# Attention per head over all 768 queries of a batch, ahead of the experts' first lot

## The chip, the cores and the metric

The kernel runs on one core of one Trainium2 chip. The metric is the device time of one execution in microseconds; the times below are medians of several executions, and one more execution was taken by the hardware profiler, from which all rows come.

## What is computed

Clustered attention feeds two expert networks, one behind the other, all in float32:

```python
# q, k, v: (2 batches, 8 heads, 768, 64); centroids: (8, 16, 64)
q_assign = argmax(q_n @ c_n)              # the cluster of each query, k_assign alike
mask = q_assign[:, :, :, None] == k_assign[:, :, None, :]
scores = where(mask, scale * q @ k.T, -1e9)
attn = softmax(scores);  out = attn @ v
x = out.transpose(0, 2, 1, 3).reshape(1536, 512)
h = x @ w_in                              # 512 -> 2048
g = (a0 + a1*h + a2*h2 + a3*h3) / (1 + |b0|*|h| + |b1|*h2 + 1e-6)
x = g @ w_out                             # 2048 -> 512
h = (x @ w1) * (x @ w2) @ w3              # 512 -> 1024, 1024 -> 1024
return h @ w_out2                         # 1024 -> 512
```

## The kernel before

The 1536 tokens go through in four **lots** of 384 (`c` = 0 to 3; lots 0 and 1 are the two halves of batch 0). The work of a lot is:

- **Masks** (`masks`, one call for a batch): for the keys and then for the queries, squares, norms, products with the centroids and the choice of the cluster, 32x32 transposes on DVE, and a write of the mask rows to DRAM (`msk_d`). Each half of it has six DVE instructions over 128x768.
- **Attention** (`Attn`): `prep` loads a head's q and k (tile `kqr`) and splits them into two float32r parts, tiles `A` and `B`; 16 rows of `B` are mask rows from `msk_d`. `unit` takes 128 queries against all 768 keys: four score matmuls (L802), the negated maximum on DVE (L814), the exponential on ACT (L815), six transposes on PE in two lots of three (L842), each copied out by ACT (L845). A lot has 8 heads times 3 units, so the program has 96 units. `av` (L876) multiplies by v for a pair of heads, two heads side by side in the 128 columns, and divides by the sums; the result goes to `x_d` in DRAM.
- **p1** (L623 to 669): x from `x_d`, times a block of w_in, then the rational function, ten to twelve ACT and DVE instructions of 128x768 (L654 to 668) on a tile `T` of the class `et`. **p2**: w_out. **p3**: w1 and w2 and their product, into tiles of the class `ab`. **p4**: the product w3·w_out2, which the kernel computes itself at its start (**W**: `FirstW` and four `w_block`, L590 and L606, kept in DRAM as `whd`, `wld`).

Every block of weights is used once a lot. In lot 0, p1 and p2 multiply in plain float32 (kind "D", L545), and the weights, which arrive as 64-bit words, are decoded by one ACT and three DVE instructions a half block (L466 to 470) and written back as float32. In the other lots a block is loaded from there into the class `raw` (3 slots), split into two float32r parts (L501 on ACT, L502 on DVE), and each product is three float32r matmuls (L547 to 549).

Lots 0 and 2 load q and k, split k, and write k's two parts to DRAM (`k_d`, L787, L788); lots 1 and 3 read them from there (L780, L781) and load only their own q. v is loaded again for each lot. For lots 1 to 3 `av` splits x into two parts before it writes them to `x_d` (L894, L895), and p1 loads both.

All of it is planned when the program is built: `Plan` places tasks by costs and priorities and gives each buffer a slot of its class (`SLOTS`), so the order on each engine is fixed in advance, and all DMAs stand in one queue, SP's, where an entry waits for its semaphores before the next is issued. Priorities come from `windows`: in before, the planner wants 36 units along with the first W blocks, lot 0's p1 from there on, and each later lot's attention spread under the blocks of the lot ahead of it. Lot 0's p1 needs only lot 0's 24 units.

Of the kernel before, what the change touches and what calls it, by code (L numbers as in the profile page):

```python
# [13 lines left out]
ALU = mybir.AluOpType  # L14
# [7 lines left out]
    F0=('in', 'out'),  # L22
    KEEP=(),
    NORM=(4, 4, 4, 4),
    NW=(1, 4),
    AT=(1.5, 2.2083, 2.5833, 4.0, 4.0, 4.0, 4.0, 4.0, 4.0),
    M1=1,
    LEAD=(5.9, 35.7, 45.3),
    ALEAD=(23.9, 20.0),
    MLEAD=252.0,  # L30
    AOFF=3.7,
    SLOTS={'w': 6, 'raw': 3, 'y': 3, 'x': 2, 'ab': 4, 'x2': 2, 'g': 16, 'et': 3, 'E': 4, 'kqr': 1, 'A': 2, 'B': 2, 'v': 1, 'sm': 6, 'nn': 3, 's': 2, 't': 2, 'm': 2, 'sums': 2, 'rb': 1},
    WO2=-768.4,
    OFF=(-119.7, -2.0, -111.7, -148.2, -107.1, 30.6, -19.2),
    T0=-75.0,
    M0=-37.2,
# [1040 lines left out]
```

## Time and profile before

| | |
|---|---|
| median of 3 runs | 808.32 us (805.76, 808.32, 809.25) |
| the profiled execution | 805.77 us, span 804.0 us |
| PE busy | 775.6 us |
| DVE busy | 614.1 us |
| ACT busy | 555.8 us |
| DMA moved | 172.08 MB, mean 214 GB/s |

Busy time is the union of an engine's instructions. Matmuls overlap their successors, so a PE that is busy all the time is not for that reason at its highest rate; the start-to-start time of equal matmuls tells the rate. Idle time of an engine counts only where the last finisher waits for it.

### The profile page before, as it was taken

Reading aid. Unit: us, or ns where it says so; the run is one execution under the profiler, and the core shown is the slowest. Engines: PE = TensorE matmul, PEld = TensorE weight load, DVE = VectorE, ACT = ScalarE, POOL = GpSimd, SP = SyncE. Lnnn points to the kernel's source line nnn. Section 1 sums busy time; section 2 is a strip of 40 time slices with the busy share of each in tenths; the row PEclk is TensorE's granted clock in tenths of the full one; section 3 lists DMA queues with packets and bytes.
Section 4 is the critical chain, followed back from the end, with each engine's and each line's share of the span. In section 5 each row is a group of like instructions: output and inputs, shape, how many; then the busy total and the mean of one; then the engine's idle time right before and its main releaser. Section 6 shows DMA issues by size and latency. Waiting matters only on the chain.

```text
span 804.0 us, 11696 instructions
## 1 busy us (share of the span) xinstructions
PE 775.6 (96%) x4225; PEld 636.7 (79%) x4225; DVE 614.1 (76%) x842; ACT 555.8 (69%) x959; POOL 0.7 (0%) x6
## 2 busy tenths in 40 slices
PE   3998999998999999999999999999999999999998
PEld 1346655565665768888889889899999999999998
DVE  6988887659999987989999663299994399983440
ACT  4887877778797867899898755378763388663331
POOL 0000000000000000000000000000000000000000
PEclk9999999999999999999999999999999999999999
DMA  8998899998768499666777842243557343653324
GB/s 322 367 304 265 272 293 262 294 284 269 233 174 295 135 368 315 206 207 216 224 234 234 286 161 97 87 132 105 206 199 229 105 134 130 228 178 132 132 103 146
DMA packets 67641, 172.08 MB, mean 214 GB/s; under 512 B 7680, under 2 KB 29952, under 8 KB 67584
## 3 DMA queue, kind: packets, MB, share of 16 engines
q1 hardware_dynamic: 67584, 171.34, 65.2%
q8 instruction: 33, 0.54, 0.3%
q14 instruction: 24, 0.20, 0.1%
HBM read 134.88 MB, written 33.29 MB: 209 GB/s over the span
## 4 chain that ended last, share of the span: by engine, by line
PE 81%; DMA 10%; ACT 4%; DVE 3%; issue 1%; SPq 1%; ACTq 0%; DVEq 0%
PE m L547 12%; PE m L548 12%; PE m L549 12%; PE s L802 6%; PE t L842 6%; PE t L876 6%; PE m L545 5%; DMA raw<-in_w_in_dram 4%; PE s L547 4%; PE s L545 4%; PE s L549 4%; PE s L548 4%; PE m L606 2%; PE t L590 1%; DMA raw<-fin 1%
## 5 line engine op out<-in xcount | busy, mean ns | idle before, releaser
L502 DVE TENSOR_TENSOR w<-raw,w 128x1024 fp32r<-128x1024 f32 x72 | 87.9, 1222 | 60.8 <-ACT w L501 55.2
L501 ACT CAST w<-raw 128x1024 fp32r<-128x1024 f32 x72 | 75.8, 1053 | 82.0 <-PE m L548 59.7
L814 DVE TENSOR_REDUCE sm<-s 128x1 f32<-128x768 f32 x96 | 90.7, 951 | 16.9 <-PE s L802 15.9
L845 ACT COPY et<-t 128x384 f32<-128x384 f32 x192 | 87.8, 494 | 21.6 <-PE t L842 19.5
L815 ACT ACTIVATE E<-s,sm 128x768 f32<-128x768 f32 x96 | 88.2, 920 | 12.5 <-DVE sm L814 10.7
L842 PEld LDWEIGHTS t<-ident,E 128*128 128x128 f32 x576 | 68.8, 140 | 34.1 <-issue 12.1
L842 PE MATMUL t<-ident,E 128*128 128x128 f32 x576 | 86.6, 276 | 7.7 <-ACT et L845 4.4
L547 PE MATMUL m<-x,w 128*128 128x384 f32 x256 | 87.4, 341 | 0.0
L548 PE MATMUL m<-x,w 128*128 128x384 f32 x256 | 86.2, 337 | 0.0
L549 PE MATMUL m<-x,w 128*128 128x384 f32 x256 | 86.1, 336 | 0.0
L876 PE MATMUL t<-et,v 128*64 128x384 f32 x384 | 69.0, 494 | 0.0
L547 PE MATMUL s<-x,w 128*128 128x384 f32 x192 | 66.1, 345 | 0.0
L547 PE MATMUL m<-g,w 128*128 128x384 f32 x192 | 64.9, 338 | 0.0
L549 PE MATMUL s<-x,w 128*128 128x384 f32 x192 | 64.9, 338 | 0.0
L549 PE MATMUL m<-g,w 128*128 128x384 f32 x192 | 64.7, 337 | 0.0
L548 PE MATMUL s<-x,w 128*128 128x384 f32 x192 | 64.6, 336 | 0.0
L548 PE MATMUL m<-g,w 128*128 128x384 f32 x192 | 64.6, 336 | 0.0
L802 PE MATMUL s<-A 128*128 128x384 f32 x192 | 60.6, 397 | 2.4 <-ACT E L815 1.8
L466 ACT ACTIVATE y<-raw 128x512 f32<-128x512 f32 x67 | 46.0, 692 | 22.3 <-DMA raw<-in_w_in_dram 9.4
L802 PE MATMUL s<-B 80*128 80x384 f32 x192 | 49.6, 339 | 0.0
L547 PEld LDWEIGHTS m<-x,w 128*128 128x128 f32 x256 | 48.1, 188 | 1.2 <-issue 1.2
L876 PEld LDWEIGHTS t<-et,v 128*64 128x64 f32 x384 | 24.7, 136 | 29.9 <-issue 27.7
(128 smaller groups left out, 1658.3 us busy)
## 6 DMA issues: line engine op xcount, KB each, us to landing
raw<-fin SPq DMA_DIRECT2D x24, 512.0 KB, 3.3
raw<-fout SPq DMA_DIRECT2D x24, 512.0 KB, 3.3
raw<-f SPq DMA_DIRECT2D x24, 512.0 KB, 3.2
kqr<-in_kq_dram SPq DMA_DIRECT2D x16, 576.0 KB, 5.4
raw<-in_w3t_dram SPq DMA_DIRECT2D x16, 512.0 KB, 5.5
raw<-in_w_in_dram SPq DMA_DIRECT2D x16, 512.0 KB, 6.1
raw<-in_w_out_dram SPq DMA_DIRECT2D x16, 512.0 KB, 4.9
raw<-in_w_dram SPq DMA_DIRECT2D x16, 512.0 KB, 5.1
```

Source lines behind the costliest of these rows:

```text
L501: op("ACT", 0.95, lambda: nc.scalar.copy(self.hi.t, self.f.t), [(self.f, 0), (self.f, 1)], [self.hi], psp)
L502: op("DVE", 1.135, lambda: nc.vector.tensor_tensor(self.lo.t, self.f.t, f32(self.hi.t), ALU.subtract), [(self.f, 0), (self.f, 1), self.hi] ...
L545: nc.tensor.matmul(o, w.f.t[:, sl], x[0], start=first, stop=last)
L547: nc.tensor.matmul(o, w.hi.t[:, sl], x[0], start=first, stop=False)
L548: nc.tensor.matmul(o, w.hi.t[:, sl], x[1], start=False, stop=False)
L549: nc.tensor.matmul(o, w.lo.t[:, sl], x[0], start=False, stop=last)
L802: nc.tensor.matmul(p.t[:, f, 0:TC], lhs.t[0:n, q0:q0 + P], lhs.t[0:n, k0:k0 + TC], start=st, stop=not st)
L814: op("DVE", 0.865, lambda: nc.vector.tensor_reduce(mx.t, p.t[:, :, 0:TC], axis=AX.XY, op=ALU.max, negate=True), [p], [mx], OF[1])
L815: op("ACT", 0.88, lambda: nc.scalar.activation(E.t, p.t[:, :, 0:TC], AF.Exp, bias=mx.t, accum_out=sums.t[:, qt, h % 2:h % 2 + 1] if late e ...
L842: nc.tensor.transpose(t.t[:, i * P:(i + 1) * P], e[:, kt * P:(kt + 1) * P], ident)
L845: op("ACT", 0.371, lambda t=t, lot=lot: nc.scalar.copy(et.t[:, 3 * lot:3 * lot + 3, qt * P:(qt + 1) * P], t.t[:, 0:TC].rearrange("p (a b) ...
L876: nc.tensor.matmul(o.t[64 * j:64 * j + 64, 0:TC], v.t[:, kt, j, :], ets[j].t[:, kt, :], start=kt == 0, stop=kt == NKT - 1)
```

## The change

- Attention is planned for a batch instead of a lot: `Attn(b)` with 48 units, a head's six units (all 768 queries) one after the other. `prep` loads q and k of a head whole (128x1536), splits them once, and neither writes nor reads `k_d`. The mask rows of a head come in one transfer.
- `av` runs for one head; the two halves of its 128 output columns are now the two lots of the batch instead of two heads. v of a pair of heads is loaded once in a batch. The result is written unsplit to `x_d` (now 512 rows by 1536 tokens) by two transfers of 64x384.
- Lot 0's p1 follows all 48 units of batch 0 (`attend(48 * ...)`).
- p1 reads x by four transfers of 128x384, one for each pair of heads, and in lots 1 to 3 splits it itself (four ACT and four DVE instructions of 128x384 a lot).
- p1's work tile `W` moves from `T` (class `et`) to a tile of the class `raw`; p3's results move from the class `ab`, which goes, to `g` (21 slots instead of 16). `FirstW` keeps decoded w_out2 in slots of `x` and `x2`.
- The eighth p1 block of the next lot stands behind p4 (`SPLIT`=7) instead of before it. The planner's numbers are others, and two of its costs; masks of batch 0 have the first place in the queue, those of batch 1 stand later.

The diff, cut to its core:

```diff
-    SLOTS={'w': 6, 'raw': 3, 'y': 3, 'x': 2, 'ab': 4, 'x2': 2, 'g': 16, 'et': 3, 'E': 4, ...},
+    SPLIT=7,
+    SLOTS={"w": 6, "raw": 3, "y": 3, "x": 2, "x2": 2, "g": 21, "et": 3, "E": 4, ...},
...
-        x_d = dr.tile([NCH, 2, NP, P, TC], F32, name="xd")
+        x_d = dr.tile([NP, P, B * S], F32, name="xd")
...
-            tl = [Buf("ab", [P, 3, 512]) for _ in range(3)]
+            tl = [Buf(c, [P, 3, 512]) for c in cfg["W2"]]
...
-                for i, t in enumerate(xs[c]):
-                    dma(lambda t=t: f32(t.t) if len(xs[c]) > 1 else t.t, lambda i=i: x_d[c, i].rearrange("n p t -> p n t"),
-                        786432, [("x", c, p) for p in range(NP)], [t], at - 8)
+                f = xs[c][-1]
+                for p in range(NP):
+                    dma(lambda p=p: f32(f.t[:, p]) if len(xs[c]) > 1 else f.t[:, p], lambda p=p: x_d[p][:, c * TC:(c + 1) * TC],
+                        196608, [("x", c, 2 * p), ("x", c, 2 * p + 1)], [(f, p)], at - 8)
+                if len(xs[c]) > 1:
+                    hi = xs[c][0]
+                    for p in range(NP):
+                        op("ACT", 0.371, lambda p=p: nc.scalar.copy(hi.t[:, p], f32(f.t[:, p])), [(f, p)], [(hi, p)], at - 4)
+                        op("DVE", 0.469, lambda p=p: nc.vector.tensor_tensor(
+                            f.t[:, p], f32(f.t[:, p]), f32(hi.t[:, p]), ALU.subtract), [(hi, p)], [(f, p)], at - 4)
...
-            T = Buf("et", [P, 3, 2, TC])
+            T, V = Buf("et", [P, 2, 2, TC]), Buf("raw", [P, 2, TC])
...
-            if m % 4 == 0:
-                ab[c, m // 4] = [Buf("ab", [P, 4, TC], F32R) for _ in range(2)]
+            if m % 2 == 0:
+                ab[c, m // 2] = [Buf("g", [P, 2, TC], F32R) for _ in range(2)]
...
-            if first:
-                dma(lambda: r.t, lambda: kq_d[b, h, :, 0:QK], 589824, w=[r], prio=pl)
-            else:
-                dma(lambda: r.t[:, qs], lambda: kq_d[b, h, :, QK:], 196608, w=[r], prio=pl)
+            dma(lambda: r.t, lambda: kq_d[b, h], 786432, w=[r], prio=pl)
...
-                for i in range(2):
-                    dma(lambda i=i: f32(A.t[64 * i:64 * i + 64, ks]), lambda: k_d[b, h, 0], 196608, [("k", b, h, 0)], [(A, "k", i)], pl)
-                dma(lambda: f32(Bt.t[0:64, ks]), lambda: k_d[b, h, 1], 196608, [("k", b, h, 1)], [(Bt, "k")], pl)
...
-                dma(lambda: k_d[b, h, 0], lambda: f32(A.t[0:64, ks]), 196608, [(A, "k", 0)], [("k", b, h, 0)], at)
-                dma(lambda: k_d[b, h, 1], lambda: f32(Bt.t[0:64, ks]), 196608, [(Bt, "k")], [("k", b, h, 1)], at)
...
-                        nc.tensor.matmul(o.t[64 * j:64 * j + 64, 0:TC], v.t[:, kt, j, :], ets[j].t[:, kt, :],
+                        nc.tensor.matmul(o.t[64 * j:64 * j + 64, 0:TA], v.t[:, kt, h % 2, :], ets[j].t[:, kt, :],
...
-            dma(lambda: x_d[c, 0:n, pr].rearrange("n p t -> p n t"), lambda: f32(xt.t) if n == 2 else xt.t, 196608 * n,
-                [(xt, i) for i in range(n)], [("x", c, pr)], at)
+            for j in range(2):
+                c, row = 2 * b + j, 64 * (h % 2)
+                dma(lambda j=j, c=c: x_d[h // 2][row:row + 64, c * TA:(c + 1) * TA], lambda j=j: xt.t[64 * j:64 * j + 64, :],
+                    98304, [xt], [("x", c, h)], at)
...
-        windows.append(((alt(p3[c], p1[c + 1]) if c + 1 < NCH else p3[c]) + p4[c], AT[2 * c + 3] if c + 1 < NCH else 4.0))
+            windows.append((alt(p3[c], p1[c + 1][:k]) + p4[c] + p1[c + 1][k:], AT[2 * c + 4]))
...
-                attend(24 * (first[x] + 1))
+                attend(48 * (first[x] // 2 + 1))
```

The order that the planner makes of it, at three places. First **DVE around the first maximum of the first unit** (`TENSOR_REDUCE` into `sm`). In before (L814) the six instructions of a half of batch 1's masks (L426 to L430, L438) stand ahead of it and around it; L558 is a split of a W block, L785 the split of k, L467 and L468 belong to a decoding:

```order
L430 STREAM_TRANSPOSE g_464<-g_469 128x768
L467 TENSOR_SCALAR y_499<-y_499 128x512
L426 TENSOR_TENSOR g_518<-g_483,s_474 128x768
L468 SCALAR_TENSOR_TENSOR y_499<-raw_416,y_499 128x512
L427 STREAM_TRANSPOSE g_527<-g_518 128x768
L558 TENSOR_TENSOR raw_532<-t_267,w_525 128x512
L438 SCALAR_TENSOR_TENSOR g_469<-s_522,g_464 128x768
L428 TENSOR_REDUCE nn_542<-g_527 128x48
L814 TENSOR_REDUCE sm_550<-s_534 128x1
L429 TENSOR_TENSOR g_527<-g_527,nn_542 128x768
L814 TENSOR_REDUCE sm_557<-s_545 128x1
L430 STREAM_TRANSPOSE g_518<-g_527 128x768
```

Behind the change the maximum is L799, decoding L468 and L470, a W split L549, the splits of q and k L774 and L776:

```order
L468 SCALAR_TENSOR_TENSOR y_378<-w_310,y_378 128x512
L468 SCALAR_TENSOR_TENSOR y_399<-raw_365,y_399 128x512
L470 SCALAR_TENSOR_TENSOR x_381<-w_310,y_378 128x512
L470 SCALAR_TENSOR_TENSOR w_420<-raw_365,y_399 128x512
L549 TENSOR_TENSOR raw_448<-t_236,w_439 128x512
L799 TENSOR_REDUCE sm_453<-s_434 128x1
L799 TENSOR_REDUCE sm_458<-s_443 128x1
L549 TENSOR_TENSOR raw_464<-t_235,w_441 128x512
L774 SCALAR_TENSOR_TENSOR A_456<-kqr_415,A_456 64x2x384
L799 TENSOR_REDUCE sm_485<-s_469 128x1
```

Nine of batch 1's twelve mask instructions stood ahead of the first maximum; now all twelve stand behind the third head's units.

Second, **PE where lot 0's p1 begins**. In before (L545) it stands between lot 1's units (L876 is lot 1's `av`), a good while behind lot 0's last `av`:

```order
L876 MATMUL t_1609<-et_1511,v_1440 64x384
L802 MATMUL s_1650<-A_1494 128x384 x2
L802 MATMUL s_1650<-B_1492 128x384 x2
L842 MATMUL t_1659<-ident,E_1572 128x128 x3
L545 MATMUL s_1666<-x_1520,w_924 128x384 x2
```

Behind the change (p1 is L536, scores L791, transposes L813) the last instruction of batch 0's last `av` (`t_2007`) stands eight rows above these; the first `s_2091` row reads the pieces of x of heads 0 to 3, the second those of heads 4 to 7:

```order
L791 MATMUL s_2069<-A_1726 128x384 x2
L791 MATMUL s_2069<-B_1724 128x384 x2
L813 MATMUL t_2077<-ident,E_2013 128x128 x3
L813 MATMUL t_2085<-ident,E_2013 128x128 x3
L536 MATMUL s_2091<-x_1582,w_917 128x384 x2
L813 MATMUL t_2098<-ident,E_2060 128x128 x3
L813 MATMUL t_2106<-ident,E_2060 128x128 x3
L791 MATMUL s_2110<-A_1887 128x384 x2
L791 MATMUL s_2110<-B_1885 128x384 x2
L813 MATMUL t_2120<-ident,E_2075 128x128 x3
L813 MATMUL t_2126<-ident,E_2075 128x128 x3
L536 MATMUL s_2091<-x_1582,w_917 128x384 x2
```

and on **SP's queue**, behind the change, that last piece of x goes out and comes back here (`xd<-E_2040`, then `x_1582<-xd`), with a mask transfer between that waits for PE's last scores of the slot before it:

```order
L350 DMA v_2038<-in_v_dram 128x768
L350 DMA xd<-E_2040 64x384 x2
L350 DMA B_2081<-msk 16x1536
L350 DMA x_1582<-xd 128x384
L350 DMA x_1647<-xd 128x384
L350 DMA B_2081<-A_2102 64x2x384
```

The last of x moved from far ahead of its use to nineteen PE rows ahead of it.

Third, **PE at the end of a lot** (lot 1 to lot 2). In before the eighth p1 block (`s_5646`) is followed by p4's four blocks (`m_5688` is the first):

```order
L547 MATMUL s_5646<-x_4452,w_5598 128x384
L548 MATMUL s_5646<-x_4452,w_5598 128x384
L549 MATMUL s_5646<-x_4436,w_5610 128x384
L547 MATMUL m_5688<-ab_5084,w_5596 128x384
L548 MATMUL m_5688<-ab_5095,w_5596 128x384
```

Behind the change it (`s_5617`) is followed by p2, and p2's first matmul that reads its result (`g_5757`) stands 78 matmuls behind it:

```order
L539 MATMUL s_5617<-x_4574,w_5550 128x384
L540 MATMUL s_5617<-x_4606,w_5561 128x384
L538 MATMUL m_5651<-g_5111,w_5590 128x384
L539 MATMUL m_5651<-g_5124,w_5590 128x384
```

```order
L540 MATMUL m_5725<-g_5519,w_5714 128x384
L538 MATMUL m_5651<-g_5757,w_5624 128x384
L539 MATMUL m_5651<-g_5768,w_5624 128x384
```

p4's four blocks moved from behind the eighth p1 block to ahead of it.

## Rows read from the trace of the kernel before

**Rows 1.** The page's first part: busy time, share and instructions of each engine.

```profile
PE 775.6 (96%) x4225; PEld 636.7 (79%) x4225; DVE 614.1 (76%) x842; ACT 555.8 (69%) x959; POOL 0.7 (0%) x6
```

**Rows 2.** Busy time by stretch: length, PE, PEld, DVE, ACT, POOL, clock, DMA share, GB/s.

```profile
0.00:80.00 80.00, 63.49 (x286) 30.68 (x287) 66.78 (x114) 57.62 (x96) 0.70 (x6) 0.98 0.91 316
80.00:200.00 120.00, 112.95 (x590) 71.39 (x588) 92.58 (x143) 94.01 (x200) 0.00 (x0) 1.00 0.94 280
200.00:520.00 320.00, 318.46 (x1743) 254.28 (x1744) 262.87 (x366) 245.88 (x450) 0.00 (x0) 1.00 0.67 218
520.00:800.00 280.00, 280.00 (x1606) 279.97 (x1605) 191.87 (x221) 157.85 (x215) 0.00 (x0) 1.00 0.45 154
```

**Rows 3.** Groups of PE from 80 to 200 us: busy, mean ns | idle before, releasers.

```profile
L842 PE MATMUL t<-ident,E 128*128 128x128 f32 x207 | 31.7, 278 | 3.7 <-ACT et L845 3.3 <-DVE E L891 0.4
L606 PE MATMUL m<-ab,w 128*128 128x512 f32 x56 | 26.3, 593 | 0.0
L876 PE MATMUL t<-et,v 128*64 128x384 f32 x144 | 25.9, 494 | 0.0
L802 PE MATMUL s<-A 128*128 128x384 f32 x66 | 21.1, 401 | 1.9 <-ACT E L815 1.8
...
L545 PE MATMUL s<-x,w 128*128 128x384 f32 x32 | 11.6, 486 | 0.0
L863 PE MATMUL t<-ident,rb 128*128 128x128 f32 x15 | 2.6, 280 | 1.3 <-ACT et L845 1.3
L545 PE MATMUL m<-g,w 128*128 128x384 f32 x4 | 1.5, 503 | 0.0
```

**Rows 4.** The chain that ended last: start us, us, what, 60 to 210 us.

```profile
63.20 1.00 ACT E L815 x2
...
117.79 0.71 PE s L802 x4
...
120.26 1.72 PE m L606 x4
121.98 4.04 PE t L876 x24
...
158.09 0.70 PE t L842 x6
...
203.39 3.87 PE s L545 x12
```

**Rows 5.** Groups of the whole span, shapes apart: a mask step, splits, the rational function.

```profile
L426 DVE TENSOR_TENSOR g<-g,s 128x768 f32<-128x768 f32 x4 | 3.8, 951 | 2.0 <-ACT g L425 2.0
L502 DVE TENSOR_TENSOR w<-raw,w 128x1024 fp32r<-128x1024 f32 x72 | 87.9, 1222 | 60.8 <-ACT w L501 55.2 <-PE s L548 3.8 <-ACT et L656 1.1
L501 ACT CAST w<-raw 128x1024 fp32r<-128x1024 f32 x72 | 75.8, 1053 | 82.0 <-PE m L548 59.7 <-issue 11.2 <-PE s L548 5.9
L662 DVE SCALAR_TENSOR_TENSOR et<-et 128x768 f32<-128x768 f32 x32 | 30.4, 951 | 2.8 <-ACT et L660 2.4
```

**Rows 6.** Waits of ACT: waited for, us in total, times, longest.

```profile
ACT y L466 <- DMA raw<-in_w_in_dram: 9.4, 7, 2.1
```

**Rows 7.** ACT from 82 to 84 us: start us, us, what.

```profile
82.13 0.92 ACT L815 ACTIVATE E<-s,sm 128x768 f32<-128x768 f32 x1
82.93 0.21 ACT L815 ACTIVATION_READ_ACCUMULATOR E<-s,sm 128x1 f32 x1
83.02 0.88 ACT L845 COPY et<-t 128x384 f32<-128x384 f32 x2
83.75 0.71 ACT L466 ACTIVATE y<-raw 128x512 f32<-128x512 f32 x1
```

**Rows 8.** DMA issues: count, KB each, median us from issue to landing.

```profile
raw<-fin SPq DMA_DIRECT2D x24, 512.0 KB, 3.3
...
A<-kd SPq DMA_DIRECT2D x32, 192.0 KB, 4.9
...
xd<-E SPq DMA_DIRECT2D x12, 384.0 KB, 3.9
...
xd<-E SPq DMA_DIRECT2D x4, 192.0 KB, 5.5
```

More of the change, by code (lines that the diff above doesn't have):

```diff
@@ L21 @@
 CFG = dict(
[L22 to L36, printed above, removed]
+    F0=("in", "out"),
+    SPLIT=7,
+    NW=(1, 3),
+    AT=(0.0, 1.125, 2.5, 2.5, 3.6667, 4.0, 4.0),
+    M1=0,
+    LEAD=(-21.2, 10.4, -104.0),
+    ALEAD=(37.3, 148.2),
+    MLEAD=16.4,
+    AOFF=-83.5,
+    SLOTS={"w": 6, "raw": 3, "y": 3, "x": 2, "x2": 2, "g": 21, "et": 3, "E": 4, "kqr": 1, "A": 2, "B": 2, "v": 1, "sm": 6, "nn": 3, "s": 2, "t": 2, "m": 2, "sums": 2, "rb": 1},
+    WO2=-2226.6,
+    OFF=(-156.1, -36.7, -5.3, -214.6, -121.6, 36.6, -69.0),
+    T0=-329.0,
+    M0=32.1,
     AHEAD=2,
-    WR=('x', 'raw', 'w', 'w', 'raw', 'et', 'raw', 'w'),
-    WT=('w', 'raw'),
-    ROUNDS=10,
+    W2=("x", "x", "x2"),
+    WR=("x", "et", "raw", "w", "et", "w", "raw", "w"),
+    WT=("w", "raw"),
+    ROUNDS=19,
 )
@@ L513, in cost @@
         def cost(self, n):
-            return n * (0.646 if self.kind == "D" else 0.489)
+            return n * (0.645 if self.kind == "D" else 0.523)
     def moe_blk(c, n, i, src):
         full = (lambda: f_d[n][i], ("f", n, i))
-        parts = tuple((lambda j=j: s_d[n][j, i], [("s", n, i, j)]) for j in range(2))
-        keep = n in cfg["KEEP"]
         if c == 0:
-            if n in F0:
-                return Blk("D", src, full)
-            return Blk("E", src, None if keep else full, parts if keep else None)
-        if keep:
-            return Blk("S" if c == 1 and n in F0 else "L", None, full, parts)
+            return Blk("D" if n in F0 else "E", src, full)
         return Blk("S", None, full)
@@ new lines, in unit, with av, inv, tr @@
+                    [t], [(et, lot, i)], OF[4])
+            if qt == 2 * NQT - 1:
+                self.av(h, OF[5])
+        def av(self, h, at):
+            b, v = self.b, self.v[h // 2]
+            sums, rb, R = self.sums[h], Buf("rb", [P, NQT, P]), Buf("t", [P, 512])
+            def inv():
+                nc.vector.tensor_scalar(sums.t, sums.t, 1e-9, None, ALU.add)
+                nc.vector.reciprocal(sums.t, sums.t)
+            def tr():
+                for i in range(NQT):
+                    nc.tensor.transpose(R.t[:, i * P:(i + 1) * P], rb.t[:, i], ident)
+            def rows():
+                return rb.t.rearrange("p i d -> p (i d)")
+            op("DVE", 0.3, inv, [(sums, j, i) for j in range(2) for i in range(NQT)], [(sums, "r")], at)
+            op("ACT", 0.4, lambda: nc.scalar.copy(
+                rb.t.rearrange("p i (j d) -> p (i j) d", j=2),
+                sums.t.rearrange("p i (j o) -> p (i j) o", o=1).to_broadcast([P, 2 * NQT, 64])), [(sums, "r")], [rb], at)
+            op("PE", 0.327, tr, [rb], [R], at)
@@ L967, in prep_heads @@
     def prep_heads(i):
-        while state["h"] <= min(i, NCH * H - 1):
-            c, h = divmod(state["h"], H)
-            att[c].prep(h, units[state["h"] * NQT])
+        while state["h"] <= min(i, B * H - 1):
+            b, h = divmod(state["h"], H)
+            att[b].prep(h, units[state["h"] * 2 * NQT])
             state["h"] += 1
@@ L983, in attend @@
                 masks(b, mask_at[b])
-            prep_heads(c * H + h)
-            att[c].unit(h, qt, units[state["u"]])
+            prep_heads(b * H + h)
+            att[b].unit(h, qt, units[state["u"]])
             state["u"] += 1
```

207 lines of the change are left out of this document (75 added, 132 removed).

## The prediction, made before the changed kernel ran

> **What bounds the kernel now.** I read the busy time by engine first, then by stretch, then counted PE's work in the worst stretch. PE is busy 775.6 us of 804.0 [rows 1], so 28.4 us are idle. The stretches [rows 2] say where: 16.5 us (80 - 63.49) before 80 us, 7.1 us from 80 to 200, 1.5 us from 200 to 520, none to 800, and the last 3 us at the end. Behind 520 us PE runs at its pace: 1606 matmuls in 280 us, 0.174 us each. So only a change of what happens before 520 us, above all before 200, can pay, unless work is taken from PE.
>
> Busy PE hides more, since matmuls overlap. From 80 to 200 us I count work at the start-to-start pace of the chain [rows 3, 4]: 207 transposes at 0.70 for six, 24.2 us; 56 W instructions at 1.72 for four, 24.1; 144 instructions of av at 4.04 for 24, 24.2; the scores, 66 instructions of the A half, two to a unit, 33 units at 0.71, 23.4; 36 plain float32 ones of p1 and p2 at 3.87 for twelve, 11.6; 15 small transposes, 1.8. That is 109.3 us of work in 120: **10.7 us lost**. What ends PE's named waits there is ACT (et L845, E L815), and ACT in turn waits 9.4 us in all for loads of w_in [rows 3, 6]; the DMA share of the stretch is 0.94, against 0.67 and 0.45 later [rows 2]. Before 80 us DVE is busy 66.78 of 80 us, more than PE, and the first exponentials start at 63.2 us [rows 2, 4].
>
> **The change part by part.** PE's work itself doesn't change: the same 96 units, the same av (two halves of the queries side by side instead of two heads) and the same blocks. So everything lies in when work can run.
>
> *The front, to the first units.* Batch 1's masks move behind the third head. Nine of their twelve DVE instructions stood ahead of the first maximum, at 0.951 us for a step, the others being of the same shape or nearly [rows 5]: 8.6 us that the first unit no longer waits for, if DVE sets the time, as 66.78 of 80 suggests. The bound below is that W's loads now come behind four mask loads of 0.39 MB: 1.6 MB at 316 GB/s [rows 2] is 5.0 us later for PE's first W work. W's last load stands behind about as many bytes in both orders, so PE still has W's sixteen loads as its cover until some 50 us; behind that it needs units. I take **-3.5**, between -8.6 and +5.0, nearer to the gain, since after 50 us only units can fill PE.
>
> *The attention stretch.* What leaves the DMA queue is k's parts, per head of batch 0 two writes and three reads of 192 KB (0.2 MB), 7.9 MB, and the second reading of v, 1.6 MB: 9.5 MB of the 280 GB/s x 120 us = 33.6 MB of this stretch, 28%, if all of it fell there. DMA goes from 0.94 to some 0.68, and waits for decoded blocks go with it. What is late next is ACT. A unit costs it 1.62 us (82.13 to 83.75 [rows 7]). A head's four preparing copies, two of 768 columns and two of 384, cost 0.79 and 0.39 us each if they go as L501's 1.053 for 1024 [rows 5]: 2.4 a head, 0.4 a unit. So 2.0 us a unit on ACT against 0.71 + 0.70 + 4.04/6 = 2.08 on PE [rows 4], which has 27.5 us of W (sixteen instructions a block, four blocks, at 1.72 for four) and the late masks besides. ACT is close, but behind. Of the 10.7 us lost I give back **-6**; the bounds are -10.7 and 0.
>
> *The first lot's x.* Lot 0's p1 used to need 24 units and its x lay ready. Now it needs all 48, and its second instruction stands nineteen PE rows behind the last av: four score groups (2.84), nine transposes of three (3.15) and one p1 step of two products (3.87/3 = 1.29), 7.3 us of cover. The path is a DVE product (half of 0.951), the write and the read: 3.9 to 5.5 for xd<-E, 4.9 for a read of 192 KB [rows 8], 9.3 to 10.9 with the product, so PE would wait 2.0 to 3.6 us, once. On SP the x load waits for the write's landing, and ahead of it a mask transfer waits for PE's scores; queued behind both are the next head's `B<-A` and `kqr`, for which that head's scores wait. Shorter transfers in an emptier queue argue for less: **+1**, bounds 0 and +3.6. The Trainium skill, "DMA: Bandwidth & Descriptors", section "Anatomy of one DMA", gives about 2.0 us plus bytes / 436 GB/s (measured on another issuing path): an estimate of 2.2 for the write and 2.5 for the read. By it the path would be hidden and this term 0; the rows here show transfers of this size at twice that.
>
> *The end of a lot.* The eighth p1 block now follows p4, and p2 needs its result 78 matmuls later, 13.6 us at 0.174. In that time DVE has six steps of the rational function and the split of g near 0.951 us, two splits of a block (1.222) and four of x (half of 0.951) [rows 5], 6.7 + 2.4 + 1.9 = 11.0, behind about two us of ACT before the first of them. That is 13 us plus hand-overs: it just fits or just doesn't. **+1** for three lots, bounds 0 and +9 (one or two more splits in the way, three times 1.222 or 2.444). Between are also raw's three slots, below.
>
> *The rest.* x is split in p1 instead of in av, the same count of instructions; q and k are split once at double width. Both run beside a full PE: 0. If the cover went, twelve pairs at half of 0.951 would cost some 11 us; PE idles 1.5 us of 320 from 200 to 520, so it is there.
>
> Sum: -3.5 - 6 + 1 + 1 = **-7.5** on the profiled execution's 805.77 us: 798.3. That execution is the fastest of those shown; the median is 808.32, 2.55 above it. Against the median I forecast **800.8 us**.
>
> **The rivals.** (1) *It relieves what nobody waited for.* No row of PE's waits names a DMA; if the attention stretch is paced by ACT's 2.0 us a unit and the order of ACT's queue, the -6 is 0 and the rest gives -1.5: **806.8**. For it speaks that ACT's 2.0 and PE's 2.08 leave little room. Against it: ACT is busy 94 of 120 us in that stretch, and 9.4 us of its idleness are loads.
>
> (2) *Front and stretch give all.* DVE's 8.6 and DMA's 10.7 come off, the x wait and the lot's end cost 1 each: -17.3, **791.0**. For it speaks that both stretches lose to things which the change removes; against it, that PE's start at the front hangs on loads, as before.
>
> (3) *Slower: p1's tile in raw.* raw has three slots. In the stretches where p1 and p3 blocks alternate, a pair takes PE 48 matmuls, 8.4 us, so the slots offer 25 us. Two block loads hold one each for 3.3 us of transfer [rows 8], 1.053 and 1.222 of splits [rows 5], 5.6 us at least; p1's W tile holds one for about six steps near 0.951 and what ACT and DVE do between, 6 to 9 us. That is 17 to 20 of 25 instead of 11. It holds while loads are prompt. If waiting for the splits' turn stretches a load's hold from 5.6 to 9 us, the sum is over 25, loads come late and PE waits: at 0.8 us for each of 24 p1 blocks, 19 us on top of the -7.5: **820**. It decides from about 8 us a hold, or, to cancel the gain alone, 0.3 us a block. Against it: from 520 to 800 DVE and ACT are busy 192 and 158 us of 280, so turns come soon.
>
> (4) *It doesn't do what it says.* If batch 0's units still ended as late because p1 in before overlapped with attention anyway, the time is that of rival 1.
>
> **How the numbers follow.** Forecast, between 796 and 804: 0.52; rival 2 and what lies below 796: 0.13; rivals 1 and 4, 804.3 to 812.4: 0.23; rival 3, or the x wait and the lot's end at their upper bounds with nothing gained: 0.12. Half a per cent, 4.0 us, is about what a measurement of this kernel can tell from no change, so faster 0.65, same 0.23, slower 0.12. The range leaves out half of the lowest case and most of rival 3: 789 to 811.
>
> **What would show it.** The first exponential well before 63 us, and PE's idle time before 80 us under 13. From 80 us to p1's first product: DMA share near 0.7, and PE's work at the pace above within 5 us of the stretch for 120 us. At p1's start: a PE wait for x of under 2 us. At each lot's end: a PE wait for g of under 1 us, three times. Behind the last unit PE at 0.174 us a matmul; a wait of PE for w (L540's operands) or of ACT for raw would show rival 3. The forecast is wrong if the attention stretch still loses some 10 us, or if PE's pace breaks behind 430 us.

## The result: 813.0 us, 0.6% slower, and the profile after

The changed kernel takes **813.0 us** (median of 20 runs, 808.21 to 815.04), the kernel before 807.54 us beside it: a ratio of 1.0058, 95% interval 1.0043 to 1.0073. The forecast was 800.8 us in a range of 789 to 811. So the sign was wrong and the time lies 2 us above the range, in the case "slower by over 0.5%" that had been given 0.12.

The profiled execution is the fastest of the 20: 808.21 us, span 806.4 us. The first line of its page, and its busy time by stretch (columns as in [rows 2]):

```profile
PE 781.4 (97%) x4225; PEld 638.7 (79%) x4225; DVE 608.3 (75%) x826; ACT 555.5 (69%) x943; POOL 0.7 (0%) x6
```

```profile
0.00:80.00 80.00, 67.22 (x281) 34.25 (x282) 60.53 (x106) 60.31 (x108) 0.70 (x6) 0.98 0.86 294
80.00:200.00 120.00, 116.40 (x657) 74.12 (x656) 92.94 (x139) 96.28 (x201) 0.00 (x0) 0.99 0.68 215
200.00:520.00 320.00, 314.77 (x1671) 247.63 (x1671) 260.06 (x358) 235.20 (x416) 0.00 (x0) 1.00 0.53 174
520.00:800.00 280.00, 280.00 (x1606) 280.00 (x1605) 194.76 (x226) 163.22 (x220) 0.00 (x0) 1.00 0.44 151
```

Against [rows 1, 2]: PE is busy 5.8 us more, which is no gain, since its work is the same; it runs at a worse pace. The DMA share of the second stretch fell from 0.94 to 0.68, just as forecast, and PE is busy 3.4 us more there. From 200 to 520 us it is busy 3.7 us less than before. Behind 520 us PE is busy all the time in both.

Busy time hides pace, so I count PE's **loss** in every stretch as in the prediction, but matmul by matmul: its length less the work that starts in it, each matmul at its start-to-start pace (about 0.43 us for a product of W, 0.32 for a plain float32 one, 0.17 for a score, an av or a float32r product, 0.11 for a transpose, 0.09 for a small product of the masks). A stretch in which PE is never idle counts a little, too, as from 440 to 800 us. (So counted, the kernel before loses 13.0 us from 80 to 200, where the prediction had 10.7 from groups.) In us:

| stretch | before | after, profiled (span 806.4) | after, once more: e1 (span 810.3) |
|---|---|---|---|
| 0 to 80 | 22.3 | 22.4 | 23.4 |
| 80 to 180 | 9.8 | 3.3 | 3.0 |
| 180 to 200 | 3.2 | 7.1 | 8.3 |
| 200 to 260 | 1.2 | 6.3 | 7.9 |
| 260 to 440 | 6.0 | 7.2 | 7.5 |
| 440 to 800 | 9.1 | 7.5 | 7.5 |
| sum | 51.6 | 53.8 | 57.6 |

So, in e1, 6.8 us are gained from 80 to 180 and 11.8 lost from 180 to 260. Each column is one execution: before's is among its fastest (805.77 us, median 807.54), e1's is near its median, so the 6.0 us between their sums are some 2 us more than the 4.1 between the medians when e1 and before were measured side by side (812.05 and 807.96). In that second stretch W's last product lies at 177.7 us and lot 0's first p1 product at 213.3 (before: 161.3 and 170.3), so for some 35 us PE has attention alone.

### The profile page after: what moved, and what is told of

It reads as the page before. It is cut to its first block, busy times and chain, and to the rows that moved or that the text cites. A ratio compares the mean times of both kernels' runs of the same rounds, so it can differ in the third digit from the quotient of the medians.

```text
span 806.4 us, 11425 instructions
## 1 busy us (share of the span) xinstructions
PE 781.4 (97%) x4225; PEld 638.7 (79%) x4225; DVE 608.3 (75%) x826; ACT 555.5 (69%) x943; POOL 0.7 (0%) x6
## 4 chain that ended last, share of the span: by engine, by line
PE 80%; ACT 7%; DVE 6%; DMA 5%; issue 1%; SPq 0%; DVEq 0%; ACTq 0%
PE m L539 12%; PE m L538 12%; PE m L540 12%; PE t L849 7%; PE s L791 6%; PE t L813 6%; PE m L536 5%; PE s L538 4%; PE s L540 4%; PE s L539 4%; PE m L597 3%; PE s L536 3%; ACT E L800 1%; DMA kqr<-in_kq_dram 1%; ACT et L816 1%
## 5 line engine op out<-in xcount | busy, mean ns | idle before, releaser
L540 PE MATMUL m<-g,w 128*128 128x384 f32 x320 | 107.9, 337 | 0.0
L538 PE MATMUL m<-g,w 128*128 128x384 f32 x320 | 107.8, 337 | 0.0
L539 PE MATMUL m<-g,w 128*128 128x384 f32 x320 | 107.7, 337 | 0.0
L799 DVE TENSOR_REDUCE sm<-s 128x1 f32<-128x768 f32 x96 | 90.3, 949 | 14.0 <-PE s L791 13.8
L813 PEld LDWEIGHTS t<-ident,E 128*128 128x128 f32 x576 | 69.2, 141 | 30.5 <-issue 11.9
L813 PE MATMUL t<-ident,E 128*128 128x128 f32 x576 | 86.4, 277 | 4.4 <-ACT et L816 3.2
L791 PE MATMUL s<-A 128*128 128x384 f32 x192 | 60.1, 394 | 6.2 <-ACT E L800 5.6
L539 PEld LDWEIGHTS m<-g,w 128*128 128x128 f32 x320 | 60.1, 188 | 0.0
L538 PEld LDWEIGHTS m<-g,w 128*128 128x128 f32 x320 | 60.1, 188 | 0.0
L540 PEld LDWEIGHTS m<-g,w 128*128 128x128 f32 x320 | 60.1, 188 | 0.0
```

The source lines that it names most:

```text
L538: nc.tensor.matmul(o, w.hi.t[:, sl], x[0], start=first, stop=False)
L539: nc.tensor.matmul(o, w.hi.t[:, sl], x[1], start=False, stop=False)
L540: nc.tensor.matmul(o, w.lo.t[:, sl], x[0], start=False, stop=last)
L791: nc.tensor.matmul(p.t[:, f, 0:TA], lhs.t[0:n, q0:q0 + P], lhs.t[0:n, k0:k0 + TA], start=st, stop=not st)
L799: op("DVE", 0.865, lambda: nc.vector.tensor_reduce(mx.t, p.t[:, :, 0:TA], axis=AX.XY, op=ALU.max, negate=True), [p], [mx], OF[1])
L813: nc.tensor.transpose(t.t[:, n * P:(n + 1) * P], e[:, kt * P:(kt + 1) * P], ident)
```

## The experiments

Theories: **A**, the dry stretch, attention without other matrix work beside it can't keep PE busy; **B**, p1's tile in raw makes block loads late (rival 3 of the prediction); **C**, a hitch, a single wait of some us, with PE at half speed behind it. Later **D**, **E** and **F** ask what sets the pace of attention alone.

**e1: the changed kernel once more.**

> The changed kernel once more, unaltered, to see an execution nearer to its median of 813.0 us than the one profiled at 808.2. In the profile at hand PE loses 13.4 us from 180 to 260 us (before loses 4.4 there) and 5.0 from 380 to 440 (before 1.7). Theory A (the dry stretch: from W's last product near 180 to lot 0's first p1 product at 213 there is nothing but attention for PE to do): 811 to 815, the extra time again lies between 180 and 260. Theory B (p1's tile in raw makes block loads late): the extra time lies behind 260, in the stretches where p1 and p3 alternate. Theory C (one hitch at 188, where a W piece waits for its slot and the granted clock falls to 0.91): the extra time lies between 185 and 205 at a lower granted clock, nothing elsewhere.

812.05 us, ratio 1.0056 (1.0034 to 1.0078). Busy time of this execution by stretch, with the granted clock behind POOL's numbers:

```profile
180.00:190.00 10.00, 6.71 (x40) 5.24 (x39) 6.47 (x11) 8.09 (x20) 0.00 (x0) 0.96 0.66 200
190.00:200.00 10.00, 10.00 (x44) 5.61 (x43) 6.73 (x9) 6.94 (x13) 0.00 (x0) 0.70 0.79 232
230.00:240.00 10.00, 8.01 (x35) 5.08 (x33) 8.57 (x12) 6.57 (x12) 0.00 (x0) 1.00 0.45 125
240.00:250.00 10.00, 9.97 (x40) 7.23 (x41) 7.75 (x10) 8.34 (x16) 0.00 (x0) 0.83 0.15 37
```

and of the kernel before:

```profile
180.00:190.00 10.00, 9.23 (x52) 5.25 (x51) 9.37 (x14) 9.92 (x18) 0.00 (x0) 1.00 0.99 310
190.00:200.00 10.00, 8.81 (x42) 5.94 (x40) 8.58 (x13) 7.04 (x15) 0.00 (x0) 1.00 0.82 244
```

PE idles 3.3 us of the first ten and is then "busy" all of the next ten, at a clock of 0.70: part of it at 1.2 GHz instead of 2.4, 3.0 us of work gone. The same again at 230 (2.0 us idle) and 240 (0.83, 1.7 us). With 0.4 at 180 that is 5.1 us; the profiled execution of after, with 0.92 and 0.91 in these first two rows and 1.00 in the others, lost 1.7 so. The 3.4 us between are most of the 3.9 by which the spans differ. After's 20 executions point the same way: the nine with a mean granted clock of 0.992 or less have a median of 814.5 us, the eleven above it 812.0. Before has such a place as well (0.69 from 64 to 68 us, behind a wait of 1.8), and its 20 executions spread by 7.6 us, after's by 6.8. The extra time of e1 lies where A and C want it, from 180 to 260, and not where B does. The Trainium skill, "TensorE: Matmul & The Clock Gate", Part 1, says that the hardware sets PE's clock by how busy it has lately been; the trace agrees (0.70 behind 3.3 us of idling).

What happens at 182 us, in the timelines of e1's SP queue, DVE, ACT and PE (start us, us, instruction, in brackets what it waited for):

```profile
182.15 0.37 SPq L350 DMA_DIRECT2D whd<-w  x1
...
182.90 0.68 DVE L549 TENSOR_TENSOR raw<-m,w 128x512 fp32r<-128x512 f32 x1
187.01 0.69 DVE L470 SCALAR_TENSOR_TENSOR w<-raw,y 128x512 uint32<-128x512 uint32 x1 [3.43 <-DMA whd<-w]
187.62 0.95 DVE L799 TENSOR_REDUCE sm<-s 128x1 f32<-128x768 f32 x1
...
188.61 0.90 ACT L800 ACTIVATE E<-s,sm 128x768 f32<-128x768 f32 x1 [1.92 <-DVE sm L799]
...
185.99 0.61 PE L791 MATMUL s<-A 128*128 128x384 f32 x2 [0.35 <-ACT E L800]
...
189.65 1.01 PE L791 MATMUL s<-A 128*128 128x384 f32 x2 [2.04 <-ACT E L800]
```

A decoded block of w_in (L470) goes into a slot of class w that still holds a W piece on its way to DRAM (`whd`). DVE stands 3.43 us, and behind L470 in its queue stands a maximum; the exponential waits for that, and PE's scores for the exponential. The same pair of score matmuls takes 0.61 us before and 1.01 us behind.

**e2: a slot of its own for the W pieces.** The order is the same as after's; the last four pieces' high parts share one new slot.

```diff
+        own.append(wt[0])
...
+    for b in own[4:]:
+        b.slot = 6
```

> Same order on every engine; the high part of the last four W pieces gets a slot of its own, so that the decoding at 186 us, for which the maxima behind it on DVE wait, no longer needs a W piece's write to DRAM to have landed. Theory C: the PE wait of 2.1 us at 188.5 and the half-speed stretch behind it go, 3 to 4 us, so 809 to 810. Theory A: the dry stretch has other hitches, at most 1 us comes off, 812 to 813. Theory B: 813, nothing changes.

812.7 us, 1.0053 (1.0029 to 1.0077): nothing. But the hitch hadn't gone, it had moved; waits from 178 to 215 us (waited for: total us, times, longest):

```profile
PE t L814 <- ACT et L817: 3.4, 2, 3.2
...
ACT w L549 <- DMA whd<-w: 2.8, 1, 2.8
```

The second piece now waits, on ACT, for the first piece's write. So e2 says nothing against C.

**e3: p1's tile out of raw.** Same order; W lies in its `et` tile as before, and the planned raw tile is never allocated.

```diff
-            T, V = Buf("et", [P, 2, 2, TC]), Buf("raw", [P, 2, TC])
+            T, V = Buf("et", [P, 3, 2, TC]), Buf("raw", [P, 2, TC])
+            inet.append(V)
...
-                return V.t
+                return T.t[:, 2]
...
+    for b in inet:
+        b.t = b
```

> Same order on every engine; p1's tile W lies in its et tile again, as in the kernel before, and the raw slots hold loads alone. Theory B: waits of ACT for raw and PE's losses from 380 to 440 (5.0 us against 1.7 before) go, and what the lots behind it lose: 807 to 810. Theories A and C: at most 1 us, 812 to 813.

812.25 us, 1.005 (1.003 to 1.007); PE's loss from 260 to 440 us is 7.0 instead of 7.5, that from 380 to 440, which B names, 4.2 instead of 4.7 (before 1.8). B falls; what loses the 2.9 us there stays open.

**e4: W held back.** Planned anew, with the last two W blocks behind heads 4 and 6.

```diff
+    HOLD = {6: [("x", 0, 4)], 7: [("x", 0, 6)]}
...
-                op("PE", 1.74, lambda j0=j0: q(j0), blk.reads([j0 * P]) + w2[j0:j0 + 2], [o], at)
+                op("PE", 1.74, lambda j0=j0: q(j0), blk.reads([j0 * P]) + w2[j0:j0 + 2] + HOLD.get(m, []), [o], at)
```

> Planned anew: the W blocks of rows 6 and 7 may not start before x of heads 4 and 6 of batch 0 is written, so W's products last until lot 0's p1 begins, and the stretch with little but attention (and batch 1's masks) lies from 90 to 130 us instead. Theory A: the loss of 180 to 260 falls from 13 to 4 to 6 us, some of it comes back at 90 to 130, so 804 to 809. Theory B: 813, since p1's tile is where it was. Theory C: 809 to 813, the slot of a W piece can be short at any place.

819.56 us, 1.0136 (1.0113 to 1.0159): the time no theory had, the mechanism A's. Busy time in the old dry stretch and in the new one, first of after (profiled), then of e4:

```profile
100.00:160.00 60.00, 60.00 (x351) 36.10 (x350) 49.88 (x73) 49.26 (x100) 0.00 (x0) 1.00 0.65 206
180.00:215.00 35.00, 30.76 (x174) 20.80 (x174) 21.54 (x33) 26.69 (x61) 0.00 (x0) 0.95 0.60 192
```

```profile
100.00:160.00 60.00, 53.70 (x343) 33.70 (x343) 49.99 (x74) 54.06 (x113) 0.00 (x0) 1.00 0.57 183
180.00:215.00 35.00, 34.71 (x188) 22.25 (x187) 18.53 (x27) 26.04 (x58) 0.00 (x0) 1.00 0.51 159
```

In these rows PE is full, or nearly so, where W stands beside attention and idle 6.3 of 60 us where W was taken away; the loss from 180 to 260 is 5.2 instead of 16.2, that from 80 to 180 is 14.2 instead of 3.0 (and 4.9 more come from 260 to 440). Matrix work that PE can put beside attention (filler, from here on) was moved, and the loss moved with it; at the new place, with batch 1's masks, it cost more. The whole order was planned anew, so e4 doesn't change the filler alone.

**e5: the last two W pieces in empty slots.** Same order; both parts of both pieces lie in g slots that nothing uses from 131 to 350 us.

```diff
+        own.append(wt)
...
+    for wt, slots in zip(own[6:], ((16, 18), (11, 17))):
+        for b, slot in zip(wt, slots):
+            b.cls, b.slot = "g", slot
```

> Same order on every engine; both parts of the last two W pieces lie in slots of the class g that stand empty from 131 to 350 us, so no decoding waits for a piece's write to DRAM and (other than in e2_wslot, where both pieces shared one slot and the wait moved to ACT, 2.8 us) no piece waits for another. Theory C (one hitch and the half-speed stretch behind it): the loss of 8.3 us from 180 to 200 falls to 2 to 3, no granted clock under 1.00 before 230, so 806 to 808. Theory A (dry stretch: attention alone can't keep PE busy): the next small wait takes the place of this one, at most 2 us off, 810 to 812.

**807.76 us**, 0.9994 (0.9975 to 1.0012): 4.3 us less than e1 by the medians, 5.0 by the two ratios, since e1 and e5 were each measured beside before, at different times; level with the kernel before. DVE at the place of the hitch, and the stretches of e5:

```profile
186.19 0.68 DVE L550 TENSOR_TENSOR g<-m,g 128x512 fp32r<-128x512 f32 x1
186.79 0.68 DVE L470 SCALAR_TENSOR_TENSOR w<-raw,y 128x512 uint32<-128x512 uint32 x1
187.39 0.95 DVE L800 TENSOR_REDUCE sm<-s 128x1 f32<-128x768 f32 x1
```

```profile
180.00:190.00 10.00, 8.74 (x50) 6.51 (x49) 8.67 (x13) 9.93 (x23) 0.00 (x0) 1.00 0.82 255
190.00:200.00 10.00, 9.96 (x60) 5.77 (x59) 7.96 (x11) 8.27 (x17) 0.00 (x0) 1.00 0.83 262
```

L470 and the maximum follow without a gap, the clock stays at 1.00, and 110 matmuls start in 20 us where e1 had 84. C holds for 180 to 200: the loss falls from 8.3 to 3.7. From 200 to 260 us 6.1 remain (before 1.2). The profiled execution is the slowest of e5's ten (811.39 us): it loses 25.7 us before 80 and 9.9 from 260 to 440, where e1 lost 23.4 and 7.5. So that the stretch's gain reaches the end is read from the medians, not from this trace.

**e6: the hitch at 239 us too.** e5, and on ACT two copies of transposes ahead of two steps (L653 and L655, the list `late`) of lot 0's second p1 block.

```diff
+    for t in late:
+        i = done.index(t)
+        j = next(n for n in range(i + 1, len(done)) if done[n].eng == "ACT")
+        done.insert(j, done.pop(i))
```

> As e5_pieces, and on ACT two copies of transposes stand ahead of two steps of the second p1 block's function (PE waited 1.3 and 0.7 us for them at 239 us in e1_again, with the granted clock at 0.83 behind it). Theory C in its wider form (each hitch of over a us costs its idle time and as much again at half speed): 3 us less than e5_pieces, 803 to 805, no clock under 1.00 from 180 to 260. Theory A: the same as e5_pieces within 1 us.

807.25 us, 0.9979 (0.9959 to 1.0): 0.5 us less than e5, and 6.1 us lost from 200 to 260, as in e5. That is what A said. In e5's trace the clock was 1.00 there already, so the half-speed stretch that C counted on wasn't there to gain.

**e7 and e9: as many bytes put back as were removed.** 96 copies of 192 KB from DRAM to DRAM, which nothing waits for: in e7 six in a row behind each head's `B<-A` (first diff), in e9 one behind every transfer while some of a head's six are owed (second diff).

```diff
+                for n in range(6):
+                    nc.sync.dma_start(out=k_d[b, h, n], in_=kq_d[b, h, 0:64, 0:S])
```

```diff
+            owed += [(b, h, n) for u, b, h in heads if u is t for n in range(6)]
+            if t.eng == "SP" and owed:
+                b, h, n = owed.pop(0)
+                nc.sync.dma_start(out=k_d[b, h, n], in_=kq_d[b, h, 0:64, 0:S])
```

> The changed kernel with six copies of 192 KB from DRAM to DRAM added for each head, which nothing waits for: 1.2 MB a head, as much as the writes and reads of k's parts and the second reading of v that the change removed. If the DMA relief is what brought PE's loss from 80 to 180 us from 9.8 to 3.0 us, as the prediction has it, that loss returns to 7 to 10 and the time is 817 to 820. If the wider spacing of W or the smaller number of preparations did it, the loss stays at 3 to 4 and the time at 811 to 814.

> As e7_traffic, but the same 96 copies of 192 KB stand one by one between the other transfers of the queue instead of six in a row, so no transfer waits behind more than one of them (in e7_traffic, 851.5 us, a head's six put about 1.2 MB ahead of whatever came next). If the DMA relief is what the stretch from 80 to 180 us gained, PE's loss there goes from 3.0 to 7 to 10 us and the time is 817 to 822. If bytes alone do little and the rows in a burst were the harm, the loss stays at 3 to 5 and the time at 812 to 815.

e7: 851.53 us, 1.0516 (1.047 to 1.0563). e9: 828.31 us, 1.0254 (1.0239 to 1.0269). Both are worse than any theory had. From 80 to 180 us, first before, then after, then e9:

```profile
80.00:180.00 100.00, 94.92 (x500) 60.21 (x499) 74.62 (x117) 77.05 (x169) 0.00 (x0) 1.00 0.94 281
```

```profile
80.00:180.00 100.00, 99.91 (x566) 62.75 (x565) 78.71 (x118) 81.47 (x170) 0.00 (x0) 1.00 0.67 213
```

```profile
80.00:180.00 100.00, 94.25 (x518) 58.28 (x518) 74.92 (x114) 76.63 (x159) 0.00 (x0) 0.98 0.81 266
```

PE's loss in this stretch is 9.8 before, 3.0 in e1, 11.7 in e9 (16.1 in e7), and e9 loses 7.3 more from 200 to 260 than e1. The step between is the wait of ACT for the weights that it decodes, from 80 to 180 us; before, after and e9:

```profile
ACT y L466 <- DMA raw<-in_w_in_dram: 7.7, 6, 2.1
...
ACT y L466 <- DMA raw<-in_w3t_dram: 0.7, 1, 0.7
```

```profile
ACT y L466 <- DMA raw<-in_w_in_dram: 1.4, 1, 1.4
...
ACT y L466 <- DMA raw<-in_w3t_dram: 1.1, 2, 0.5
```

```profile
ACT y L466 <- DMA raw<-in_w_in_dram: 7.6, 3, 3.6
...
ACT y L466 <- DMA raw<-in_w3t_dram: 4.9, 3, 2.8
```

8.4 us went to 2.5 with the change and to 12.5 with the copies, PE's loss from 9.8 to 3.3 and to 11.7. So, with the same work and, but for the copies, the same order, traffic alone takes the gain away, by the path that the prediction named. That the relief is worth just 6.8 us isn't shown: the copies are other transfers than those that were removed, they bring the DMA share to 0.81 and not to 0.94, and the spacing of W and the masks changed with the relief. The place in the queue counts besides the bytes: the same copies in rows of six cost 39.5 us over e1, one by one 16.3 (37 and 16 by the ratios).

**e8: lot 0's p1 free of attention.** Planned anew; its x comes from q.

```diff
-                    ... lambda p=p: x_d[p][:, c * TC:(c + 1) * TC],
+                    ... lambda p=p: x_d[p][:, c * TC:(c + 1) * TC] if c else kq_d[0, p][:, 0:TC],
-                        196608, [("x", c, 2 * p), ("x", c, 2 * p + 1)], [(f, p)], at - 8)
+                        196608, [("x", c, 2 * p), ("x", c, 2 * p + 1)] if c else [], [(f, p)], at - 8)
...
-            if x in first:
+            if x in first and first[x]:
                 attend(48 * (first[x] // 2 + 1))
```

> Planned anew with lot 0's p1 free of attention: its x is read from the input q instead (its result isn't the reference's), so p1's blocks may start when the planner likes, and come about 15 us of PE work earlier, just behind the last W block. It prices the wait for all 48 units. Theory A: PE loses 4 to 7 us from 160 to 260 instead of 13 to 17, so 802 to 807. Theory C: the slot of a W piece is as short as before, 809 to 813.

810.04 us, 1.0018 (1.0 to 1.0036): C's range, but not C's reason, since the planner's new order has no hitch at W's pieces (180 to 200 loses 3.6). p1 starts at 199.0 instead of 215.9 and W's last product lies at 180.5, so the dry stretch is half as long; and yet 200 to 260 still loses 6.4, as in e5 (6.1) with p1 waiting for all units. So an earlier start of p1 alone didn't bring the time back. One reason can be counted in the traces: from 200 to 260 us before starts 119 products of p1 and p2 beside 36 score matmuls and loses 1.2, e8 only 77 beside 44, e1 64 beside 52. So e8 put the filler earlier, but thinner than before. That this is why it loses more is read from the counts, not tested; p1's results stand in the same two `s` slots as the scores, which is a rival.

**e10 and e11: is it ACT's load?** Theory D is rival 1 of the prediction, for attention alone: in e6 ACT is busy 17.82 of 20 us there. One of a unit's two copies of transposes goes from ACT to DVE, for units 40 to 59 (e10) and also 0 to 19 (e11).

```diff
+                u = 48 * self.b + 6 * h + qt
+                copy = nc.vector.tensor_copy if lot and (40 <= u < 60) else nc.scalar.copy
-                op("ACT", 0.371, lambda t=t, lot=lot: nc.scalar.copy(
+                op("ACT", 0.371, lambda t=t, lot=lot, copy=copy: copy(
```

> e6_pieces_act with one of the two copies of transposes of each of the units 40 to 59 on DVE instead of ACT, same order. From 180 to 200 us ACT is busy 17.8 of 20 us in e6_pieces_act, DVE 16.6, PE loses 4.4; from 180 to 240 together 9.6. Theory D (with nothing but attention beside it, ACT's share of a unit is what PE waits for: rival 1 of the prediction, in the stretches without W work): 0.45 us a unit off ACT, the loss of 180 to 240 goes to 4 to 6 and the time to 802 to 804. Theory E (the chain from score to maximum to exponential to transposes has only two slots of s, and its length sets the pace): 806 to 808, and worse if the copies delay maxima on DVE.

> As e10_dvecopy, with the units 0 to 19 too; from 60 to 80 us ACT is busy 19.7 of 20 us in e6_pieces_act and PE loses 3.7 there, 4.1 from 40 to 60. Theory D: 2 to 4 us less than e10_dvecopy, 799 to 802, and it is this, not the order of the masks, that the prediction's -3.5 for the front missed. Theory E: the same as e10_dvecopy or up to 2 us more.

810.16 us, 1.0025 (1.0009 to 1.0041), and 812.89, 1.0068 (1.005 to 1.0085): 2.9 and 5.6 us worse than e6. First e6, then e10:

```profile
180.00:200.00 20.00, 18.48 (x108) 12.01 (x107) 16.63 (x25) 17.82 (x40) 0.00 (x0) 1.00 0.87 258
200.00:220.00 20.00, 19.27 (x110) 13.16 (x110) 10.20 (x16) 16.56 (x38) 0.00 (x0) 1.00 0.41 135
```

```profile
180.00:200.00 20.00, 18.55 (x109) 12.26 (x108) 18.40 (x29) 16.75 (x35) 0.00 (x0) 1.00 0.87 263
200.00:220.00 20.00, 18.35 (x112) 12.76 (x111) 15.21 (x26) 14.21 (x30) 0.00 (x0) 1.00 0.44 145
```

ACT has 3.4 us less to do in these 40 and PE loses no less (180 to 260: 11.5 against 10.5; before 80 us e11 loses 24.3, e6 24.8). D's gain didn't come. But the edit moved the load and didn't remove it: DVE is busy 6.8 us more in these 40, and from 180 to 260 a new wait of PE for DVE's copies of 2.8 us stands beside its waits for ACT, which fall from 3.0 to 2.1. So copies on DVE don't pay, and whether ACT's load alone would pace attention stays open.

**e12: four t slots instead of two.** e6, with the two tiles of class m, idle from 180 to 230 us, as t slots besides.

```diff
+    for b in sorted(plan.queue["t"], key=lambda b: span[b]):
+        if LO <= span[b][0] < HI:
+            b.cls, b.slot = k = min((k for k in free if free[k] < span[b][0]), key=free.get)
+            free[k] = span[b][1]
```

> e6_pieces_act with four slots for the transposes' results instead of two between lot 0's last W piece and its p2 (about 180 to 230 us): the two banks of class m, which nothing uses there, serve as well; same order. What is left open is which wait sets the pace of attention alone, where PE loses 9.6 us from 180 to 240 in e6_pieces_act; e10_dvecopy showed that it isn't ACT's load. If it is the copies that keep the two t slots (theory F), PE's waits for et go, the loss is 5 to 7 and the time 803 to 805. If it is the two s slots, held through maximum and exponential (theory E), PE's next wait is for E instead, the loss stays within 1 us and the time at 806 to 808.

807.5 us, 0.9981 (0.9961 to 1.0001): as e6. Waits of PE and its weight loads from 180 to 240 us, e6 and then e12:

```profile
PEld s L795 <- ACT E L804: 3.7, 8, 0.7
PEld t L817 <- ACT et L820: 3.4, 7, 1.0
...
PE s L795 <- ACT E L804: 1.6, 4, 0.5
PE t L817 <- ACT et L820: 1.4, 3, 0.8
```

```profile
PEld s L796 <- ACT E L805: 4.2, 8, 1.1
...
PE s L796 <- ACT E L805: 2.1, 4, 0.9
...
PE s L796 <- DVE et L662: 1.6, 1, 1.6
...
PE t L818 <- ACT et L821: 0.3, 1, 0.3
```

The waits for t go from 1.4 to 0.3 and come back as waits for `s`, for the exponential or for p1's function to let go of it; the loss from 180 to 240 is 10.8 (e6: 9.6). F falls. The waits and the time are what E forecast. A third `s` slot wasn't tried, so E isn't shown by taking its cause away.

## Why the prediction was wrong, step by step

Its terms against e1, whose time is near the median (one trace on each side):

| step | forecast | measured (loss, e1 less before) |
|---|---|---|
| front, to 80 us | -3.5 | +1.1 |
| attention stretch, as far as W lasts (80 to 180) | -6 (meant for 80 to 200) | -6.8 |
| start of lot 0's p1 (180 to 260) | +1 (x alone) | +11.8 |
| lots' ends, rest (260 to 800) | +1 | -0.1 |
| sum | -7.5 | +6.0 |

**The step that failed** is that of the attention stretch together with the first lot's x. The prediction took W's 27.5 us, and the late masks, as PE's filler up to p1's first product, and priced p1's later start as a wait for x alone, +1. W's last product came 36 us ahead of p1, and from 180 to 260 us PE lost 11.8 us more than before. In the prediction's own stretch, 80 to 200, the -6 was -1.7 (13.0 to 11.3), so its own sign of being wrong, "still loses some 10 us", came true.

**As long as W lasts, the step was right** in direction and path: to 180 us the DMA share went to 0.67, ACT's waits for weights from 8.4 us to 2.5, and e9 takes the gain away by traffic alone. That -6.8 is so near -6 is in part luck, since the -6 was meant for a longer stretch.

**The front.** The step held literally and brought nothing: the first exponential starts 8.2 us earlier than in [rows 4], where 8.6 was forecast.

```profile
54.95 0.88 ACT L800 ACTIVATE E<-s,sm 128x768 f32<-128x768 f32 x1
```

PE's idle time before 80 us fell from 16.5 to 12.8, under the 13 that was set as a sign, but the loss didn't. The step took "the first unit no longer waits" for "PE does more by 80 us". Before loses 5.4 us from 60 to 80, most of it in three waits around 64 us (0.50, 1.77 and 0.57) with a clock of 0.69 from 64 to 68; after loses 3.5 and 3.2 from 40 to 60 and from 60 to 80 in small ones. By 50 us 58 of W's 128 products had started (before 51), and batch 1's masks, some 8 us of PE work, had been moved behind them. The units came earlier into a PE that had less to put beside them. That this is the reason is read from the traces; the front alone wasn't changed in a run.

**The x wait.** Forecast +1, measured 0, in after's timeline of DVE, SP's queue and PE:

```profile
208.76 0.56 DVE L857 TENSOR_TENSOR E<-t,rb 128x384 f32<-128x384 f32 x1 [0.50 <-PE t L849]
...
209.35 1.09 SPq L350 DMA_DIRECT2D xd<-E  x2
...
213.13 0.85 SPq L350 DMA_DIRECT2D x<-xd  x2
...
216.84 1.46 PE L536 MATMUL s<-x,w 128*128 128x384 f32 x4
```

From the product's start to PE's use pass 8.1 us without a wait of PE for x. The path's transfers took, from 175 to 220 us, 2.9 us (write) and 2.5 us (read) in the median; the term had been sized from [rows 8] at 3.9 to 5.5 and 4.9; the four writes at 5.5 all lie where the DMA share was 0.94, the others are medians of the whole kernel before. Over the whole program the two medians are:

```profile
xd<-E SPq DMA_DIRECT2D x32, 96.0 KB, 3.3
x<-xd SPq DMA_DIRECT2D x16, 192.0 KB, 3.1
```

The other rule that the prediction weighed, the Trainium skill, "DMA: Bandwidth & Descriptors", section "Anatomy of one DMA", gives some 2.2 us for 96 KB and 2.5 for 192 KB as an estimate (about 2.0 us plus bytes / 436 GB/s, measured on another issuing path). It was nearer to this stretch than those rows, and by it the term would have been the 0 that came.

**What the runs showed in its place.** The stretch from 180 to 260 came out 10.8 us above its term. I looked at the wait that the later start of p1 could cause and not at what is left for PE to do while attention waits for itself. Two costs lie there. One is the hitch at 188: a W piece, a decoded block and a maximum meet in slots of w and in DVE's queue. Its price with the half-speed stretch behind it is 4.3 us (e1 to e5, medians; 5.0 by the ratios); it alone makes the difference between level and slower. The other is the rest, some 5.4 us in e5 (9.8 us lost from 180 to 260 against 4.4). It is not that one wait (e6) and not the t slots (e12), and copies on DVE don't cure it (e10); where e4 has W as filler it is gone, and an earlier but thin p1 doesn't take it away (e8). Whether ACT's load or the two `s` slots set the pace of attention alone stays open.

**The rivals.** Rival 1 said that ACT's 2.0 us a unit would pace the attention stretch and the -6 be 0: as far as W lasts, the 6.8 us gained speak against it; behind W it isn't excluded, since e10 and e11 put ACT's load on DVE. Rival 3 had the right sign for a wrong reason: e3 takes its mechanism out and nothing comes of it. The lots' ends cost nothing: among after's waits of PE none of 0.4 us or more is for p2's g, and from 520 to 800 us PE is busy 280.00 of 280 us, as before. (The bound of +9 for them isn't what its working gives: three times 2.444 is 7.3.)

None of these versions is clearly faster than the kernel before: e6 and e12 are 0.2% under before, with intervals that reach to 1.0.

## What to carry to other kernels

When work is reordered, look not only for the wait at the new seam but for the stretch that is left without other work: there small waits are paid, and one may be paid nearly twice (in e1 3.3 us of idling with 3.0 us of half speed behind). A slot shared by a result on its way to DRAM and by the next block's decoding stalls whatever stands behind that decoding in the engine's queue; such results need free slots of their own, or the wait only changes engines (e2 and e5). And a start that comes earlier is no gain by itself; ask what the engine that bounds the kernel has left to put beside it (the front, read from the traces and not tested).

## What the runs showed of the hardware that I had not expected

The granted clock of PE fell behind single gaps of about 2 us (2.04 in e1 at 190 us, 1.77 in before at 64 us), and not alike in each execution of the same program: from 180 to 190 and 190 to 200 us it was 0.92 and 0.91 in after's profiled execution, 0.96 and 0.70 in e1; behind the wait of 1.3 us at 239 us it was 0.83 in e1 and 1.00 in e5. And 18.9 MB of copies that nothing waits for, 11% of all bytes moved in e9, cost 16 us one by one and 39 in rows of six, although the DMA share stays below that of the kernel before (0.81 against 0.94 from 80 to 180 us).
